# Moving weight conversions, parked stores and late casts within the step order of a retention + two-layer MLP kernel

## The chip, the cores and the metric

One core of one Trainium2 chip runs the whole program. The metric is the device time in microseconds of one execution, as the median over runs. The engines are named as in the profile: PE (matmul), PEld (weight load), DVE (VectorE), ACT (ScalarE), POOL (GpSimd), SP (SyncE, which issues nearly all transfers).

## What is computed

```python
x = attention_with_decay(q, k, v)           # 4 x 8 heads, 576 x 64 each, no softmax
x = x.transpose(0, 2, 1, 3).reshape(2304, 512)
h = x @ w_in                                # 512 -> 2048
x = (h * sigmoid(1.702 * h)) @ w_out        # 2048 -> 512
h = x @ w2_in                               # 512 -> 1024
h = h * softmax(h); h = layer_norm(h) * g_ln
out = h @ w2_out                            # 1024 -> 512
```

## The kernel before

**The stages.** Attention for 16 units of heads comes first, then the first MLP, which the change is about, then the second MLP. Every product of the two MLPs is made of three fp32r matmuls: an operand is held as a rounded part and the rest (`split`: ACT casts, POOL subtracts), and high x high, low x high and high x low are summed.

**The 24 steps.** The first MLP goes through the 2048 hidden columns in four generations `g` of 512. In each generation it goes through three token pairs (768 tokens each, forwards in an even generation, backwards in an odd one), and for each pair through two halves `i` of the generation's columns. This gives the steps s = 6g + 2 * (place of the pair) + i. A step has an h part (`emit_h`) and a y part (`emit_y`). The h part is seven products of six matmuls, in the order A, C, B, A again, C again, D, B again, on four PSUM banks of the ring "s". ACT copies A to c11 (L715) and C to c22 (L719) before the second A and C may be added to the same banks; DVE makes c12 = B + c11 (L707) before the second B. Then come the sums on DVE and four gates, called g11, g12, g21 and g22 in this order: ACT writes the rounded gate and the full one, and POOL (DVE in steps 1 and 3) subtracts them for the low part (L681). The y part is four units of 12 matmuls, each on the 'low' and the 'high' part of one gate. In generation 0 the y parts have other lengths: step 1 has 48 matmuls, step 3 has 72, step 5 has 24. In an even step of the later generations the y part is that of the pair's other half of tokens from the step before, so in these the gates of the step itself are used one step later. DVE adds four finished y banks to memory at the end of a y part (L782).

**The reloading steps.** The operands x of a pair are seven tiles of 768 KB. In the later generations the second step of a pair (7, 9, 13, 15, 19, 21) issues on SP the load of tile j of the next pair (`load_x`, L668) as soon as product j of the pair has read the old one. In steps 1 and 3 the tiles of the next pair are cast and subtracted instead (`split(j)`) and stored to DRAM.

**The background queue.** All weights arrive as 64-bit numbers and have to be made into fp32 by three DVE instructions (`convert`, L276 to L278). These conversions (cost 3), sums of weight blocks on DVE (cost 0.5 for the combinations of the first MLP, L283; cost 1 for those of the second, `v` in `queue_w2in`) and splits stand in one list, `bg`, in a fixed order. A call `slot(n)` takes items from its head until n is used up. An item with a cost that is not ready, because of its `need`, stops the list; an item without cost that isn't ready goes to `held` and is looked at again in the next call. Items marked late run at the head of a later call, at most three (LATE) in each. A split marked "spill" makes an operand of the second MLP in a parking tile (`park`), and its store to DRAM goes out on SP at the end of the call; one such store is allowed in a call, and none while `quiet` is set. A conversion also issues on SP, behind itself, the load of the piece after next into the buffer that it has read (L262), so a load waits on SP until its conversion is done, and what is issued on SP after it waits as well.

**The calls.** In each step there is `slot(0)` behind g11 in the middle of the h part, `slot(pace(s, 0))` at the end of the h part ("h slot" below) and `slot(pace(s, 1))` at the end of the y part ("y slot"). `pace` is a table for the first six steps (PACE), and after that spreads the rest of the list over the calls in proportion to a table `most` with a row for each step of a generation. Before step 23 `flush` calls `slot(9)` until all is done. A conversion writes to a PSUM bank of ring "s", or of ring "y" where `ring` or `psum` says so.

Of the kernel before, what the change touches and what calls it, by code (L numbers as in the profile page):

```python
# [21 lines left out]
DM = H * D  # L22
# [87 lines left out]
_M = {}  # L110
# [44 lines left out]
class Build:  # L155
# [141 lines left out]
    def slot(self, n):  # L297


        late, self.late, i = self.late, [], 0  # L300
        for x in late:
            fn, give, spill = x
            if i >= LATE or (spill and (self.quiet or len(self.stores) > self.last)):
                self.late.append(x)
                continue
            if fn is not None:
                fn()
                i += 1
            self.done.add(give)
        ready = lambda need: all(x in self.done for x in need)  # L310
        wait, self.held = self.held, []
        for x in wait:
            if ready(x[2]):
                self.begin(*x)
            else:
                self.held.append(x)
        while self.bg:
            cost, _, need, _, _ = self.bg[0]
            if cost and (n <= 0 or not ready(need)):
                break  # L320
            x = self.bg.pop(0)
            if ready(need):
                self.begin(*x)
                n -= cost
            else:
                self.held.append(x)
        for fn in self.stores:
            fn()
        self.stores = []
# [16 lines left out]
    def pace(self, s, part):  # L346


        if s < len(PACE):
            return PACE[s][part]  # L350
        most = lambda t, b: ((6, 3), (6, 0), (6, 3), (6, 0), (6, 6), (6, 6))[t % 6][b]
        room = sum(most(t, b) for t in range(s, NSTEP - 1) for b in range(2) if (t, b) >= (s, part))
        return min(most(s, part), -(-self.left() * most(s, part) // room)) if room else 0

# [93 lines left out]
    def queue_w2in(self, c):  # L448

        s = lambda k: self.at(W2_AT[k], DM)  # L450
        before = lambda k: (("r", c - 1, k),) if c else ()
        for k in W2IN:
            self.next_raw(W2_AT[k], before(k))
        v = lambda o, a, b, need=(): self.add(1, lambda: self.sub(s(o), s(a), s(b)), need)
        v(4, 1, 0, before(4) + before(5))
        v(1, 3, 1)
        self.queue_spill(("b11", c), s(0), ("b11", c))
        self.queue_spill(("b22", c), s(3), ("b22", c))
        self.queue_spill(("t1", c), s(4), ("r", c, 5))
        self.queue_spill(("t3", c), s(1), ("r", c, 1))  # L460
        v(0, 3, 4, (("b11", c),))
        self.add(0, lambda: self.done.add(("r", c, 4)))
        v(3, 2, 0, (("b22", c),))
        self.queue_spill(("b21", c), s(2), ("r", c, 2))
        self.queue_spill(("t2", c), s(0), ("r", c, 0))
        self.queue_spill(("t4", c), s(3), ("r", c, 3))


    def un(self, u):
# [215 lines left out]
    def emit_h(self, s):  # L685
# [4 lines left out]
        n = 2 * g + i  # L690
# [35 lines left out]
        yield 2  # L726
        mul(A, 3, "b21", False, True)
        g11(A)
        self.slot(0)
        yield 3  # L730
        mul(C, 4, "b22", False, True)
        add(C, C, c12)
# [203 lines left out]
    def prepare(self):  # L936
# [6 lines left out]
        for i in range(2):  # L943
            self.wo[i] = slot(self.wop, f"wo{i}", SLICE, F32R)
        late_in = [slot(self.wop, f"wo{i}", SLICE, U32) for i in (2, 3)]
# [35 lines left out]
        self.add(0, lambda: swap("win1"))  # L981
        self.queue_convert(late_in[0], _M["stg"], (("in", 0),), None, self.ybank)
        self.queue_in(1, (), slice(0, 1))
        self.queue_convert(late_in[1], _M["stg"] + DM, (("in", 0),))
        self.queue_combine()
        self.add(0, lambda: [swap(2), swap(3)])
        self.queue_in(1, (), slice(1, 3))
# [14 lines left out]
    def run(self):  # L1002
# [15 lines left out]
        def load_w():  # L1018
            dst, piece = self.first_loads.pop(0)
            self.load_raw(dst, self.source(piece))  # L1020
# [22 lines left out]
        for k in range(NPAIR):  # L1043
# [4 lines left out]
            if k == 0:  # L1048
                pt, ends, o = self.bank("T0"), None, []
# [28 lines left out]
            else:  # L1078
# [5 lines left out]
                o, ends = [self.bank(f"o{u}")], [self.bank(f"e{k}")]  # L1084
# [34 lines left out]
        for g, p, i in STEPS:  # L1119
            s = 6 * g + 2 * PAIRS[g].index(p) + i  # L1120
# [7 lines left out]
            for j in self.emit_h(s) if s else chain([0], steps):  # L1128
                while s == 0 and self.first_loads:
                    load_w()  # L1130
                if s == 0:
                    self.store_x(p, j)
                if s == 1 and j == 3:
                    for fn in sums[2:]:
                        fn()
                if s == 2 and j == 4:
                    sums, split = self.combine_x(PAIRS[0][2])
                    for fn in sums:
                        fn()
                if i and after is not None:  # L1140
                    if g == 0:
                        split(j)
                        self.store_x(after, j)
                    else:
                        self.load_x(after, j)
# [31 lines left out]
            self.done.add(("y", s))  # L1177
            self.ring = self.bank if g == 0 and i == 0 else self.ybank
            self.quiet = g > 0 and i == 0 and at + 1 < NPR
            self.slot(self.pace(s, 1))  # L1180
            self.quiet, self.ring = False, self.bank
            if s == 0:
                self.slot(0)
        for fn in y1[:6] + y2[:4]:
            fn()
        self.emit_y(GENS - 1, PAIRS[-1][-1], 1, range(NF - FG, NF))
# [125 lines left out]
```

## Time and profile before

| | |
|---|---|
| median of 3 runs | 670.05 us (669.88 to 671.6) |
| profiled execution | 669.62 us, span 667.8 us |
| PE busy | 647.0 us (97%) |
| DVE, ACT, POOL busy | 447.0 us (67%), 284.5 us (43%), 306.4 us (46%) |
| mean granted clock of PE | 0.992 |
| first step of the first MLP to first matmul of the second | 63.46 to 464.43 us |
| transfers | 121.78 MB, mean 182 GB/s |

Times in the trace count from the start of the span. Busy PE means that matmuls are under way; at a lower granted clock the same matmuls are busy for longer. Granted clock 1.00 is the level of 2.4 GHz, and a mean between 0.5 and 1 over a stretch means that a part of it was run at 1.2 GHz.

### The profile page before, as it was taken

Reading aid. Unit: us, or ns where it says so; the run is one execution under the profiler, and the core shown is the slowest. Engines: PE = TensorE matmul, PEld = TensorE weight load, DVE = VectorE, ACT = ScalarE, POOL = GpSimd, SP = SyncE. Lnnn points to the kernel's source line nnn. Section 1 sums busy time; section 2 is a strip of 40 time slices with the busy share of each in tenths; the row PEclk is TensorE's granted clock in tenths of the full one; section 3 lists DMA queues with packets and bytes.
Section 4 is the critical chain, followed back from the end, with each engine's and each line's share of the span. In section 5 each row is a group of like instructions: output and inputs, shape, how many; then the busy total and the mean of one; then the engine's idle time right before and its main releaser. Section 6 shows DMA issues by size and latency. Waiting matters only on the chain.

```text
span 667.8 us, 11310 instructions
## 1 busy us (share of the span) xinstructions
PE 647.0 (97%) x4326; PEld 601.6 (90%) x4326; DVE 447.0 (67%) x744; ACT 284.5 (43%) x614; POOL 306.4 (46%) x314
## 2 busy tenths in 40 slices
PE   9998989899999999999999999899999999999998
PEld 8997979899999989999999989899888888888887
DVE  3789868737657557557566535345798987887780
ACT  3564553835434324334434434242445433543331
POOL 3687584867246625354735434234244322431200
PEclk9998989899999999999999999999999999999999
DMA  8999356472495943494932584759400000000001
GB/s 348 418 418 373 142 205 252 165 262 66 155 354 198 348 172 97 151 368 164 406 106 85 175 357 164 325 163 365 201 17 32 18 17 31 33 17 16 32 31 49
DMA packets 30006, 121.78 MB, mean 182 GB/s; under 512 B 3328, under 2 KB 3840, under 8 KB 29952
## 3 DMA queue, kind: packets, MB, share of 16 engines
q1 hardware_dynamic: 29808, 120.99, 47.8%
q8 instruction: 34, 0.56, 0.3%
q14 instruction: 20, 0.16, 0.1%
q10 hardware_dynamic: 144, 0.07, 0.0%
HBM read 88.28 MB, written 32.77 MB: 181 GB/s over the span
## 4 chain that ended last, share of the span: by engine, by line
PE 80%; DVE 8%; DMA 8%; issue 2%; ACT 2%; SPq 0%; DVEq 0%; ACTq 0%
PE y L773 23%; PE o L927 15%; PE h L837 13%; DMA x<-xd 8%; PE h_B L701 6%; PE h_A L701 6%; PE h_C L701 6%; DVE mem L283 3%; PE h_D L701 3%; PE zT L901 2%; PE s L570 2%; PE o L585 1%; DVE mem L575 1%; PE warm L1013 1%; PE T L534 1%
## 5 line engine op out<-in xcount | busy, mean ns | idle before, releaser
L681 POOL TENSOR_TENSOR g<-mem,g 128x384 fp32r<-128x384 f32 x86 | 89.4, 1054 | 161.3 <-ACT mem L680 161.2
L292 POOL TENSOR_TENSOR win<-mem,win 128x256 fp32r<-128x256 f32 (+2 forms) x59 | 53.6, 934 | 56.1 <-ACT win L291 52.0
L773 PE MATMUL y<-g,wo 128*128 128x384 f32 x432 | 78.0, 334 | 0.0
L773 PEld LDWEIGHTS y<-g,wo 128*128 128x128 f32 x432 | 75.1, 188 | 0.3 <-DVE mem L782 0.2
L707 DVE TENSOR_TENSOR mem<-h_B,mem 128x384 f32<-128x384 f32 x48 | 26.7, 556 | 64.7 <-PE h_B L701 63.5
L782 DVE TENSOR_TENSOR mem<-y,mem 128x384 f32<-128x384 f32 x76 | 38.5, 551 | 35.5 <-PE y L773 35.2
L283 DVE TENSOR_TENSOR mem<-mem 128x256 f32<-128x256 f32 (+2 forms) x49 | 42.9, 905 | 7.1 <-POOL ws L292 6.4
L292 POOL TENSOR_TENSOR ws<-mem,ws 128x512 fp32r<-128x512 f32 (+1 forms) x32 | 36.8, 1159 | 18.4 <-ACT ws L291 14.2
L715 ACT COPY mem<-h_A 128x384 f32<-128x384 f32 x24 | 11.5, 479 | 77.9 <-PE h_A L701 77.9
L658 POOL TENSOR_TENSOR x<-mem,x 128x384 fp32r<-128x384 f32 x42 | 43.5, 1070 | 0.0
L837 PE MATMUL h<-ut,win 128*128 128x512 f32 x168 | 42.9, 391 | 0.0
L888 POOL TENSOR_TENSOR mem<-mem 128x1 f32<-128x1 f32 x18 | 10.3, 572 | 68.8 <-DVE mem L887 62.6
L927 PE MATMUL o<-u,zs 128*128 128x512 f32 (+1 forms) x171 | 41.7, 388 | 0.0
L773 PE MATMUL y<-g,wo0dt.float32r 128*128 128x384 f32 x216 | 40.3, 334 | 0.0
L773 PE MATMUL y<-g,wo1dt.float32r 128*128 128x384 f32 x216 | 40.3, 334 | 0.0
L927 PE MATMUL o<-wo,zs 128*128 128x512 f32 (+1 forms) x171 | 40.0, 378 | 0.0
L843 DVE TENSOR_TENSOR mem<-h,mem 128x512 f32<-128x512 f32 x36 | 24.6, 687 | 22.4 <-PE h L837 12.5
L773 PEld LDWEIGHTS y<-g,wo0dt.float32r 128*128 128x128 f32 x216 | 37.7, 188 | 0.0
L773 PEld LDWEIGHTS y<-g,wo1dt.float32r 128*128 128x128 f32 x216 | 37.7, 188 | 0.0
L837 PEld LDWEIGHTS h<-ut,win 128*128 128x128 f32 x168 | 31.4, 188 | 6.4
L927 PEld LDWEIGHTS o<-wo,zs 128*128 128x128 f32 x171 | 31.0, 188 | 6.0
L927 PEld LDWEIGHTS o<-u,zs 128*128 128x128 f32 x171 | 29.9, 189 | 5.2
(154 smaller groups left out, 1518.2 us busy)
## 6 DMA issues: line engine op xcount, KB each, us to landing
x<-xd SPq DMA_DIRECT2D x42, 768.0 KB, 8.9
xd<-x SPq DMA_DIRECT2D x21, 768.0 KB, 3.7
mem<-in_w SPq DMA_DIRECT2D x28, 512.0 KB, 4.9
in<-in_att SPq DMA_DIRECT2D x16, 576.0 KB, 7.7
in<-in_att SPq DMA_DIRECT2D x16, 544.0 KB, 8.0
out<-mem SPq DMA_DIRECT2D x17, 256.0 KB, 2.0
mem<-in_w2in SPq DMA_DIRECT2D x8, 512.0 KB, 3.8
wdt<-ws SPq DMA_DIRECT2D x8, 512.0 KB, 8.4
```

The source lines that it names most:

```text
L283: self.nc.vector.tensor_tensor(o, a, b, ALU.subtract)
L292: self.nc.gpsimd.tensor_tensor(lo, src, f32(hi), ALU.subtract)
L570: nc.tensor.matmul(s[a][:, c * CH:(c + 1) * CH], t[h, k:k + CH], self.q(t, c, h), start=True, stop=True)
L658: (engine or self.nc.gpsimd).tensor_tensor(x[:, 1, k], a[:, k], f32(x[:, 0, k]), ALU.subtract)
L681: engine.tensor_tensor(gs[:, 1], u, f32(gs[:, 0]), ALU.subtract)
L701: nc.tensor.matmul(o, w[:, c:c + P], x[j][:, m, k], start=(start and i == 0), stop=(stop and i == 5), skip_group_check=True,)
L707: add = lambda o, a, b: nc.vector.tensor_tensor(o, a, b, ALU.add)
L773: nc.tensor.matmul(o[m], w[:, c:c + P], gs[:, b], start=(begin and i == 0), stop=(end and i == 2),)
L782: nc.vector.tensor_tensor(y[:, m], o[m], y[:, m], ALU.add)
L837: nc.tensor.matmul(o, a[:, l, k], w[:, m], start=(start and i == 0), stop=(stop and i == 5), skip_group_check=True,)
L843: add = lambda o, a, b: nc.vector.tensor_tensor(o, a, b, ALU.add)
L927: nc.tensor.matmul(o[:, 0:n], z[:, a, k], w[:, b, p * n:(p + 1) * n], start=(k == 0 and i == 0), stop=(k == FB - 1 and i == 2),)
```

## The change

Five things are changed. Items of cost 1 no longer stop the list: a sum that isn't ready is held like the items without cost, and the names that the spills and sums of `queue_w2in` wait for are given by the sums themselves. The table `most` has 0 in place of 3 for the y slots of the first and the third step of a generation. The calls behind g11 are quiet, so they make no spill. In generation 0 the y slots of steps 2 and 4 are left out, and of step 0's two calls at the end the second goes to step 1, behind the second product. The conversion of the second late input piece uses ring "y".

```diff
@@ slot
-            if cost and (n <= 0 or not ready(need)):
+            if cost and cost != 1 and (n <= 0 or not ready(need)):
                 break
@@ pace
-        most = lambda t, b: ((6, 3), (6, 0), (6, 3), (6, 0), (6, 6), (6, 6))[t % 6][b]
+        most = lambda t, b: ((6, 0), (6, 0), (6, 0), (6, 0), (6, 6), (6, 6))[t % 6][b]
@@ queue_w2in
-        v = lambda o, a, b, need=(): self.add(1, lambda: self.sub(s(o), s(a), s(b)), need)
+        def v(o, a, b, need=(), give=None):
+            self.add(1, lambda: self.sub(s(o), s(a), s(b)), need, give)
+
         v(4, 1, 0, before(4) + before(5))
         v(1, 3, 1)
...
-        v(0, 3, 4, (("b11", c),))
-        self.add(0, lambda: self.done.add(("r", c, 4)))
-        v(3, 2, 0, (("b22", c),))
-        self.queue_spill(("b21", c), s(2), ("r", c, 2))
-        self.queue_spill(("t2", c), s(0), ("r", c, 0))
-        self.queue_spill(("t4", c), s(3), ("r", c, 3))
+        v(0, 3, 4, (("b11", c),), ("r", c, 4))
+        v(3, 2, 0, (("b22", c), ("r", c, 4)), ("v", c))
+        self.queue_spill(("b21", c), s(2), ("r", c, 2), (("v", c),))
+        self.queue_spill(("t2", c), s(0), ("r", c, 0), (("v", c),))
+        self.queue_spill(("t4", c), s(3), ("r", c, 3), (("v", c),))
@@ emit_h
         g11(A)
+        self.quiet = True
         self.slot(0)
+        self.quiet = False
@@ prepare
-        self.queue_convert(late_in[1], _M["stg"] + DM, (("in", 0),))
+        self.queue_convert(late_in[1], _M["stg"] + DM, (("in", 0),), None, self.ybank)
@@ run, in the loop over the products of a step
+                if s == 1 and j == 1:
+                    self.slot(0)
@@ run, end of a step
-            self.slot(self.pace(s, 1))
+            if s not in (2, 4):
+                self.slot(self.pace(s, 1))
             self.quiet, self.ring = False, self.bank
-            if s == 0:
-                self.slot(0)
```

## Rows read from the trace of the kernel before

**Rows 1.** Windows, each from one step's first matmul to the next's: steps 1, 3, 5, 9, 10, 16, 20, 22

```profile
core 0: us, PE busy (x) PEld busy (x) DVE busy (x) ACT busy (x) POOL busy (x), PEclk, DMA share, GB/s
83.88:105.72 21.84, 19.19 (x91) 16.99 (x91) 14.03 (x20) 12.22 (x24) 19.20 (x17) 0.92 0.65 251
117.16:141.42 24.26, 21.90 (x116) 21.16 (x115) 15.61 (x24) 15.52 (x31) 21.93 (x20) 0.93 0.54 217
152.86:165.81 12.95, 11.74 (x68) 11.43 (x68) 9.40 (x16) 6.87 (x15) 9.81 (x9) 1.00 0.26 81
212.71:228.31 15.60, 15.60 (x92) 15.60 (x92) 11.61 (x20) 7.74 (x16) 14.64 (x12) 1.00 0.75 271
228.31:247.31 19.00, 16.63 (x92) 15.43 (x92) 7.81 (x15) 4.34 (x10) 4.00 (x4) 1.00 0.68 272
325.31:342.21 16.90, 16.08 (x91) 15.50 (x91) 7.79 (x15) 4.34 (x10) 7.24 (x7) 1.00 0.72 289
389.01:406.62 17.61, 16.33 (x92) 15.46 (x91) 6.74 (x13) 4.35 (x10) 3.98 (x4) 1.00 0.64 257
422.22:440.31 18.09, 16.32 (x91) 15.45 (x91) 6.73 (x13) 5.69 (x12) 5.28 (x5) 1.00 0.53 216
```

**Rows 2.** Timeline of PE: product groups after a wait, in steps 1, 3, 5, 10

```profile
89.38 1.79 PE L701 MATMUL h_A<-x,win1dt.float32r 128*128 128x384 f32 x6 [1.84 <-ACT mem L715]
...
123.08 1.48 PE L701 MATMUL h_A<-x,win1dt.float32r 128*128 128x384 f32 x6 [2.06 <-ACT mem L715]
...
157.35 1.34 PE L701 MATMUL h_A<-x,win1dt.float32r 128*128 128x384 f32 x6 [1.21 <-ACT mem L715]
...
237.87 1.28 PE L701 MATMUL h_B<-x,win 128*128 128x384 f32 x6 [0.56 <-DMA x<-xd]
```

**Rows 3.** Windows over the 24 matmuls that follow the first three of these waits

```profile
89.38:95.21 5.83, 5.83 (x25) 5.83 (x26) 3.04 (x4) 4.03 (x7) 5.83 (x6) 0.71 0.67 246
123.08:128.94 5.86, 5.86 (x25) 5.76 (x25) 2.24 (x5) 5.86 (x11) 5.86 (x6) 0.71 0.44 149
157.35:161.65 4.30, 4.30 (x25) 4.30 (x26) 1.29 (x3) 2.58 (x6) 4.20 (x4) 1.00 0.39 122
```

**Rows 4.** Timeline of SP: x loads of step 7; weight load and x loads of step 9

```profile
182.74 2.40 SPq L668 DMA_DIRECT2D x<-xd  x3
...
216.59 0.33 SPq L262 DMA_DIRECT2D mem<-in_w  x1
217.01 2.25 SPq L668 DMA_DIRECT2D x<-xd  x3
```

**Rows 5.** DMA issues: the x load issued at 222.62, us to landing last

```profile
x<-xd SPq DMA_DIRECT2D x1, 768.0 KB, 15.1
```

**Rows 6.** Timeline of DVE: sums in steps 6, 8 and 11; conversion and c12 in step 12

```profile
179.08 1.41 DVE L283 TENSOR_TENSOR mem<-mem 128x512 f32<-128x512 f32 x2
...
208.29 4.36 DVE L283 TENSOR_TENSOR mem<-mem 128x256 f32<-128x256 f32 x4
...
248.27 0.75 DVE L283 TENSOR_TENSOR mem<-mem 128x256 f32<-128x256 f32 x2
...
263.87 0.68 DVE L276 TENSOR_SCALAR conv<-mem 128x512 uint32<-128x512 uint32 x1
...
268.25 0.55 DVE L707 TENSOR_TENSOR mem<-h_B,mem 128x384 f32<-128x384 f32 x1
```

**Rows 7.** Timeline of ACT: casts in step 1; scaling of a parked operand in step 22

```profile
88.33 0.62 ACT L291 CAST wo3dt.float32r<-mem 128x512 fp32r<-128x512 f32 x1 [1.51 <-DVE mem L278]
...
90.32 1.58 ACT L656 CAST x<-mem 128x768 fp32r<-128x768 f32 x2
...
435.97 0.73 ACT L290 ACTIVATE mem<-mem 128x512 f32<-128x512 f32 x1 [0.95 <-DVE mem L278]
```

**Rows 8.** Timeline of POOL: low part of g11 in step 4; weight splits in step 5

```profile
146.73 1.02 POOL L681 TENSOR_TENSOR g<-mem,g 128x384 fp32r<-128x384 f32 x1 [6.11 <-ACT mem L680]
...
153.05 1.48 POOL L292 TENSOR_TENSOR win0dt.float32r<-mem,win0dt.float32r 128x512 fp32r<-128x512 f32 x1
...
156.48 3.09 POOL L292 TENSOR_TENSOR win0dt.float32r<-mem,win0dt.float32r 128x768 fp32r<-128x768 f32 x2 [1.95 <-ACT win0dt.float32r L291]
```

## The prediction

> **What bounds the kernel now.** I read the page first: PE is busy nearly all the time, so only its gaps, and matmuls at a lower clock, can be won. I then cut the first MLP into windows from one step's first matmul to the next's. A step without a loss takes 15.60 us for 90 matmuls, 0.173 us each, and PE is busy in all of it [rows 1]; a product of six takes 1.04. Against this count, step 1 (90 matmuls) loses 6.2 us, step 3 (114 matmuls, 19.8 us) loses 4.5 and step 5 (66 matmuls, 11.4 us) loses 1.5. Steps 10, 16, 20 and 22 lose 3.40, 1.30, 2.01 and 2.49 us, together 9.20 [rows 1]. The other later steps were at 15.6 in the timeline. The two groups have different causes.
>
> In steps 1, 3 and 5 the second A waits 1.84, 2.06 and 1.21 us for ACT's copy of the first A [rows 2]. ACT is late since weight casts stand in front of the copy, and these wait for DVE: the cast of wo3 ended its wait for a conversion at 88.33 [rows 7]. Behind the first two waits PE also ran slower: 24 matmuls took 5.83 and 5.86 us at a granted clock of 0.71, so part of them at the 1.2 GHz level, and behind the third 4.30 at 1.00 [rows 3]. 24 at full rate are 4.16, so the clock cost 1.67 and 1.70, and nothing to speak of behind the 1.21 wait.
>
> In the other four, PE waits for x, as at 237.87 [rows 2]. These loads went out one step earlier. Step 7 begins 31.2 us (two steps) before 212.71, at 181.5, and its first x load goes out at 182.74, 1.2 us in; in step 9 it goes out at 217.01, 4.3 us in, just behind a weight load that SP could issue only at 216.59 [rows 1, 4]. The last x load of step 9 was issued at 222.62 and landed 15.1 later, at 237.7 [rows 5]: 20.7 us from the first issue to the last landing. The second B of step 10, which needs it, was due 15.60 + 6 x 1.04 = 21.84 us after the start of step 9, at 234.55. Started at 1.2 us, the same transfers end at 21.9 even at step 9's slow rate. So the late start decides, and behind it that a conversion stands in front of the x loads on SP.
>
> **Where the change puts things.** I followed the list by its rules through all 24 steps. (1) The y slots of steps 8, 14, 18 and 20, which converted one piece each in front of steps 9, 15, 19 and 21, convert nothing. Their pieces go into h slots (steps 9, 14, 19, 21), behind the x loads on SP or finished before them, and the stores that g11's slot put between x loads go to later slots. (2) The late casts in front of steps 1, 3 and 5 run behind the second product (step 1) or behind g11 (steps 3 and 5). (3) What was spread has to go somewhere: the h slot of step 10 gets four combinations where it had two, the y slot of step 10 two conversions, the y slot of step 11 two conversions and two sums, the h slot of step 12 two conversions behind a sum that waits for POOL, and the last two conversions reach step 22, one in each slot. The parked operand of the very last piece is therefore made in the flush in front of step 23, where the flush was empty before.
>
> **Costs.** *Reloads:* x starts at about 1.2 us in steps 9, 15, 19 and 21, so all four losses go: -9.20. Step 13 had a clean start; now two weight loads stand in front of it, the second issued about 2 us in, which puts its x loads at about 3 us. With 18 to 19 us to the last landing (step 9's 20.7 with a 512 KB store among them) that is 21 to 22 against 21.84: 0, at most 1.9 with the full 20.7.
>
> *Step 1:* the copies and x casts pass the wo3 cast, but everything that follows on ACT (x casts, g11, and behind them DVE's sums and g12) still waits for the same conversion. In the old order the copy of A, one x cast and the copy of C lie between wo3's cast, whose next instruction starts about 0.5 after it, and the x casts at 90.32 [rows 7]; 90.32 - 88.85 = 1.47 is what the chain wins. The wait of PE moves from the h part to the y part, where g12 is late, and with it the lower clock. I take -1.4 out of 6.2; bounds 0 and -3.1, the chain's 1.47 plus the 1.67 of the clock.
>
> *Step 3:* the wait of 2.06 and the 1.70 of clock go. D's bank is that of step 2's last conversion, which ends some 0.3 us behind the time at which D would be due: -3.76 + 0.3 = -3.45.
>
> *Step 5:* the three casts now stand on POOL between g11's low part and g12's. The low part of g11 starts 5.31 into a step (146.73 in step 4, which began at 141.42) [rows 1, 8]. Then 1.02 + 1.48 + 3.09 + 1.02 give 11.9 at step 5's own prices [rows 8]. The y part of step 5 needs g12's low at 7.28 + 2.08 + 0.69 = 10.05. PE waits 1.85, and a little less where POOL is alone, say 1.7, in place of the 1.5 lost now: +0.2. The cover that a y part gives elsewhere (three units, 6.2 us) is missing in this short one. A wait of 1.7 is nearer to 1.84, which cost the clock, than to 1.21, which didn't [rows 2, 3]: +1.7 (bounds 0 and 1.7).
>
> *DVE between steps 10 and 13:* in step 12 (start 247.31 + 15.60 = 262.91) two conversions ran in front of c12 from 263.87 to 268.25, and c12 ended at 268.80, in time for the second B due at 269.15 [rows 1, 6]. Two sums of 512 columns, 1.41 [rows 6], now stand between: c12 ends at 270.2, +1.1. Step 11 gets the same two conversions behind two more combinations, which take 0.75 to 2.2 (two at 0.75, four at 4.36) [rows 6]; some of that is covered by the wait for y's last bank: 0 to 0.7, I take 0.5.
>
> *Step 23:* the conversion in front of it starts 0.96 into the step and ends about 2.2 later [rows 6], at 3.2. ACT then scales (0.73) and casts (about 0.5 to the next start) [rows 7], and copies A: 4.9 to 5.0. The second A is due at 3.12, so PE waits 1.8: +1.8, and by the row of the 1.84 wait +1.7 of clock [rows 2, 3]. SP's store of that piece holds up the loads of the second MLP's weights by some 6 us; these have the 17 us of two y parts as cover, and cost nothing unless they are held beyond that.
>
> *Nothing:* the quiet call in the other steps, the held sums (DVE stands idle in front of c12 in most steps), and step 0's bank of ring "y", whose gain of some 0.6 us ends in step 1's wait for the same conversions.
>
> **Sum:** -9.20 - 1.4 - 3.45 + 0.2 + 1.7 + 1.1 + 0.5 + 1.8 + 1.7 = -7.05. From the profiled execution's 669.62 that gives 662.6; the median of the runs is 0.43 above that execution, so 663.0.
>
> **Rivals.** *A, the new waits cost no clock:* in steps 5 and 23 PE waits but goes on at 2.4 GHz, as behind the wait of 1.21. That speaks for it in step 5, the 1.84 row against it in step 23. Both: 663.0 - 3.4 = 659.6.
>
> *B, the reload is mended in part:* the x loads start early, but the weight loads and stores now bunched in h slots get between them or in front, as in step 13. If half of the 9.20 stays, 667.6. Against it speaks that step 7 starts clean behind the same kind of h slot.
>
> *C, slower:* the casts behind g11 make POOL late for g12 in steps 9, 11 and 17 too, as in step 5. There the y part needs g12's low only after three units, at 7.28 + 6.24 = 13.5, and POOL should be through by 11 to 12; it decides from 1.5 to 2.5 us of further lateness on. Each place would cost a wait and clock of about 3.4, so three make 663.0 + 10.2 = 673.2. What could make POOL late is work of DVE beside it: four sums took 4.36 us in step 8, where two took 0.75 in step 11 [rows 6]. The Trainium skill (GPSIMD Engine Reference, 8. Key points) says that GpSimd shares its SBUF interfaces with VectorE and contends with its instructions of two SBUF inputs, as these sums are. By that rule the casts put into the same stretch as DVE's work would stretch each other and rival C would be the outcome; the sums' rows agree that such a stretch occurs, but its size there, 2.9 us over four sums, was without loss to PE in step 9 [rows 1].
>
> *D, no change:* if SP is held by something else than the conversion (the store in front of the weight load), the x loads start no earlier, and -9.20 falls away while the new waits stay: 672. The clean start of step 7 speaks against it.
>
> **How the numbers follow.** A difference under 0.3% (2 us) can't be told from none. Forecast 0.58, with a range of its own from 660.5 to 665.5: the clock of one place, step 1's bound, step 13's. A 0.20. B 0.10. C 0.06, D 0.06. Faster by over 2 us is all of the forecast and of A and nearly all of B: 0.87. Within 2 us: the worse part of B, 0.04. Slower: most of C and D, 0.09. The range from 658.0 to 668.0 leaves out C and D and the best ends of A.
>
> **What would show it.** Right: no wait of PE for x in steps 10, 16, 20 and 22 and steps of 15.6 us there; step 3 at about 20.8; x loads 1.2 us into steps 9, 15, 19 and 21; a wait of about 1.8 for ACT in the second A of step 23 and one of about 1 in the second B of step 12; in step 5 a wait in the y part for POOL's g. Wrong: the second A of step 23 on time, or waits of PE for POOL in steps 9, 11 or 17; x loads of step 9 still behind a late weight load.

## The result and the profile after

The changed kernel takes 662.27 us (median of 4 runs, 661.43 to 663.43) against 669.96 of the kernel before on the same chip (669.42 to 671.6): ratio 0.9882, 95% interval 0.9859 to 0.9905. Its profiled execution took 662.16, span 660.4, at a mean granted clock of 0.997.

The first view is again windows from one step's first matmul to the next's, of steps 1, 3, 5, 9 to 12, 14, 22 and 23 (columns as in [rows 1]):

```profile
core 0: us, PE busy (x) PEld busy (x) DVE busy (x) ACT busy (x) POOL busy (x), PEclk, DMA share, GB/s
82.66:103.33 20.67, 17.91 (x91) 17.19 (x92) 14.25 (x20) 12.23 (x24) 19.72 (x17) 0.92 0.71 266
114.77:135.81 21.04, 20.48 (x115) 19.69 (x115) 14.91 (x24) 15.32 (x31) 19.52 (x18) 1.00 0.55 213
147.25:160.69 13.44, 11.71 (x67) 11.39 (x67) 10.34 (x18) 7.24 (x16) 8.35 (x8) 1.00 0.27 84
207.53:223.12 15.59, 15.59 (x91) 15.59 (x91) 8.71 (x16) 6.39 (x14) 11.12 (x10) 1.00 0.97 373
223.12:238.72 15.60, 15.60 (x91) 15.60 (x91) 10.03 (x15) 5.89 (x13) 8.00 (x7) 1.00 0.64 246
238.72:255.44 16.72, 15.90 (x91) 15.58 (x91) 14.15 (x24) 6.10 (x13) 8.66 (x8) 1.00 0.43 140
255.44:272.75 17.31, 15.88 (x91) 15.56 (x91) 12.36 (x19) 5.37 (x12) 6.96 (x6) 1.00 0.27 82
288.35:306.00 17.65, 16.34 (x91) 15.46 (x91) 13.03 (x24) 7.13 (x15) 11.01 (x10) 1.00 0.74 277
...
415.20:430.80 15.60, 15.60 (x91) 15.60 (x91) 6.73 (x13) 5.69 (x12) 5.30 (x5) 1.00 0.42 171
430.80:456.92 26.12, 24.40 (x140) 23.81 (x139) 15.95 (x29) 9.90 (x23) 12.29 (x14) 1.00 0.74 284
```

Against [rows 1], steps 10 and 22 are at 15.60, as are 16 and 20: the 9.20 us of the reloads are gone. Step 3 is 3.2 us shorter than its 24.26. Steps 11, 12, 14 and 23, which had no loss, now wait, and steps 1 and 5 wait at another place than before. The timeline of PE after shows where:

```profile
95.36 3.91 PE L776 MATMUL y<-g,wo3dt.float32r 128*128 128x384 f32 x12 [2.26 <-ACT g L679]
...
159.20 1.66 PE L776 MATMUL y<-g,wo3dt.float32r 128*128 128x384 f32 x8 [1.73 <-POOL g L682]
...
245.95 1.34 PE L702 MATMUL h_B<-x,win0dt.float32r 128*128 128x384 f32 x6 [0.82 <-DVE mem L708]
...
263.28 1.31 PE L702 MATMUL h_B<-x,win1dt.float32r 128*128 128x384 f32 x6 [1.43 <-DVE mem L708]
...
294.76 1.29 PE L702 MATMUL h_D<-x,win1dt.float32r 128*128 128x384 f32 x6 [0.56 <-DMA x<-xd]
...
435.81 1.34 PE L702 MATMUL h_A<-x,win1dt.float32r 128*128 128x384 f32 x6 [1.72 <-ACT mem L716]
```

They are the y part of step 1 (the gate's wait of 2.26), the y part of step 5, c12 in steps 11 and 12, the x of step 14, and the second A of step 23. Windows over the matmuls behind the first, second and last of these waits, to be held against [rows 3]:

```profile
95.36:99.30 3.94, 3.94 (x14) 3.94 (x15) 3.29 (x5) 3.94 (x8) 3.94 (x4) 0.57 0.91 381
159.20:163.40 4.20, 4.20 (x24) 4.20 (x25) 2.17 (x4) 3.41 (x8) 3.14 (x3) 1.00 0.57 169
435.81:439.98 4.17, 4.17 (x24) 4.17 (x25) 1.10 (x2) 2.07 (x5) 2.15 (x3) 1.00 0.41 136
```

Only behind step 1's wait is a part run at 1.2 GHz. Steps 5 and 23 go on at 2.4 GHz.

The timeline of SP after: the x loads of step 9, then in step 13 a store and the x loads behind it.

```profile
208.76 6.56 SPq L669 DMA_DIRECT2D x<-xd  x7
...
276.32 0.42 SPq L432 DMA_DIRECT2D wdb<-ws  x1
276.83 5.78 SPq L669 DMA_DIRECT2D x<-xd  x7
```

Step 9 (start 207.53) issues its first x load 1.23 us in; in step 13 (start 272.75), behind two weight loads and a store, it is 4.08.

The lengths of the steps of all kernels that were run, in us, from the same windows; a dot is 15.60 to 15.65, and steps left out (2, 4, 7, 9, 15, 17 to 19, 21) have no loss in any.

| kernel | 0 | 1 | 3 | 5 | 6 | 8 | 10 | 11 | 12 | 13 | 14 | 16 | 20 | 22 | 23 |
|---|---|---|---|---|---|---|---|---|---|---|---|---|---|---|---|
| before | 20.41 | 21.84 | 24.26 | 12.95 | 15.70 | · | 19.00 | · | · | · | · | 16.91 | 17.61 | 18.09 | 24.11 |
| after | 18.72 | 20.66 | 21.05 | 13.44 | · | · | · | 16.72 | 17.31 | · | 17.65 | · | · | · | 26.11 |
| u1 | 20.19 | 20.92 | 21.02 | 13.46 | · | · | · | · | 17.33 | 19.90 | 16.53 | · | · | · | 24.11 |
| u2 | 20.06 | 20.90 | 21.04 | 13.46 | · | 16.62 | 17.24 | · | 17.17 | 15.79 | 19.26 | · | · | · | 26.13 |
| u3 | 18.74 | 20.67 | 21.05 | 13.46 | · | · | 18.34 | · | 15.75 | · | · | 16.81 | 17.59 | 19.04 | 24.09 |
| u4 | 19.27 | 21.84 | 24.27 | 12.95 | 15.70 | · | 16.31 | · | · | · | · | · | · | · | 24.09 |
| u5 | 20.21 | 20.87 | 21.03 | 13.44 | · | · | 18.06 | · | · | · | · | · | 16.15 | · | 24.11 |
| f1 | 18.75 | 20.80 | 21.05 | 13.46 | · | · | · | 16.70 | 17.33 | · | 17.65 | · | · | · | 24.11 |
| f2 | 20.06 | 20.88 | 21.03 | 13.46 | · | · | · | · | · | · | · | · | · | · | 26.11 |
| f3 | 20.28 | 20.90 | 21.03 | 11.44 | 16.25 | · | · | 16.73 | 17.31 | · | 17.39 | · | · | · | 26.11 |
| f4 | 19.97 | 22.46 | 21.07 | 13.46 | · | · | · | 16.71 | 17.31 | · | 17.46 | · | · | · | 26.09 |
| f5 | 18.73 | 23.60 | 21.03 | 11.44 | 16.24 | · | · | · | · | · | · | · | · | · | 24.11 |
| f6 | 21.17 | 17.30 | 21.03 | 13.46 | · | · | · | 16.73 | 17.31 | · | 17.32 | · | · | · | 26.11 |
| f7 | 18.74 | 17.28 | 21.03 | 11.44 | 16.27 | · | · | · | · | · | · | · | · | · | 24.11 |

Step 0 changes by 1.1 to 1.6 us between executions whatever the edit, and by 2.4 in f6; the last section comes to it. So a difference of that size between two medians is read from the steps.

### The profile page after: what moved, and what is told of

The parts are those of the page before. It is cut to its first block, busy times and chain, and to the rows that moved or that the text cites. A ratio compares the mean times of both kernels' runs of the same rounds, so it can differ in the third digit from the quotient of the medians.

```text
span 660.4 us, 11306 instructions
## 1 busy us (share of the span) xinstructions
PE 642.1 (97%) x4326; PEld 600.3 (91%) x4326; DVE 446.4 (68%) x744; ACT 283.6 (43%) x614; POOL 305.2 (46%) x314
## 4 chain that ended last, share of the span: by engine, by line
PE 80%; DVE 11%; issue 3%; DMA 2%; POOL 1%; ACT 1%; DVEq 0%; POOLq 0%; ACTq 0%
PE y L776 25%; PE o L930 15%; PE h L840 13%; PE h_B L702 6%; PE h_A L702 6%; PE h_C L702 5%; DVE mem L283 3%; PE h_D L702 3%; PE zT L904 2%; DMA x<-xd 2%; PE s L571 2%; PE o L586 1%; DVE mem L576 1%; DVE conv L277 1%; DVE conv L276 1%
## 5 line engine op out<-in xcount | busy, mean ns | idle before, releaser
L283 DVE TENSOR_TENSOR mem<-mem 128x256 f32<-128x256 f32 (+2 forms) x49 | 46.4, 982 | 12.0 <-POOL ws L292 11.3
```

What stands on the lines that cost most here:

```text
L283: self.nc.vector.tensor_tensor(o, a, b, ALU.subtract)
```

## Experiments

Two groups: u1 to u5 take the change apart, f1 to f7 try its new waits. Diffs of u1, u2 and f1 to f7 are against the changed kernel, those of u3 to u5 against the kernel before. Ratios are to the kernel before on the same chip.

**u1: the old table back.**

```diff
-        most = lambda t, b: ((6, 0), (6, 0), (6, 0), (6, 0), (6, 6), (6, 6))[t % 6][b]
+        most = lambda t, b: ((6, 3), (6, 0), (6, 3), (6, 0), (6, 6), (6, 6))[t % 6][b]
```

> The changed kernel with the old table of work after a step's y part, so that a step in front of a reloading one may convert again; everything else stays changed. By the rules of the queue a conversion that also issues a weight load then stands in front of the x loads of steps 7, 9, 15 and 19; the one in front of step 21 issues no weight load, in front of step 13 there are four combinations and no load; and the last spill leaves before step 23. Theory (SP waits at the weight load for the conversion's end, and the x loads stand behind it): steps 8, 10, 16 and 20 lose about what before's steps 10, 16 and 20 lost (3.4, 1.3, 2.0 us; between 1 and 3.5 us each), step 22 loses nothing, step 14's 2.05 us falls as its load comes in another place, step 23 wins back its 2.0 us; about 662.3 + 4 x 2 - 4 = 666 us. Rival 1 (the conversions themselves, by VectorE's time, held the x loads): step 22 loses its 2.5 us too, 668 us. Rival 2 (the spills' stores between the x loads were the cause): no step loses, 658 us.

664.06 us (662.7 to 666.18), ratio 0.9893 [0.9826, 0.9960]. The theory fell. The conversion and its weight load stand in front of the x loads again, as the timeline of SP in step 9 (start 209.50) shows, and step 10 lost nothing; neither did 8, 16 and 20. So far rival 2 holds.

```profile
212.63 0.33 SPq L262 DMA_DIRECT2D mem<-in_w  x1
213.05 4.61 SPq L669 DMA_DIRECT2D x<-xd  x7
```

What it lost instead was in step 13, where the four combinations stood on DVE in front of c12, and PE waited 2.46 us and then ran on at the lower level:

```profile
282.49 2.24 PE L702 MATMUL h_B<-x,win 128*128 128x384 f32 x6 [2.46 <-DVE mem L708]
```

The 0.93 that step 14 lost is not for x either: the last x landed 3.84 us into the step, and the longest wait of PE there, 0.64 at its second A, was for ACT's copy.

**u2: spills, and with them stores, let in behind g11 again.**

```diff
-        self.quiet = True
         self.slot(0)
-        self.quiet = False
```

> The changed kernel without the rule that holds spills back at the place behind the first gate. One store then stands between the x loads again in steps 7, 9, 13, 19 and 21 (in before there were up to two in some), while no conversion stands in front of them. Theory (the weight load behind a conversion was the cause, a store only adds its own time on the DMA engines, about 1.2 us): steps 8, 10, 20 and 22 lose 0 to 0.5 us each, step 14's 2.05 us grows by up to 1.2 us; 662 to 664 us. Rival (the stores between the x loads held them back): half or more of 3.4, 2.0 and 2.5 us returns in steps 10, 20 and 22; 666 us or more.

665.88 us (663.4 to 667.57), ratio 0.9938 [0.9913, 0.9962]. Steps 20 and 22 stayed clean with a store between the x loads, so the store alone doesn't make the wait either. Step 10 lost 1.64, for x, and step 14 lost 1.6 more than in the changed kernel. In step 9 the first x load was also late there, 3.43 us in, behind another store that SP issued at 3.01. Step 8's 1.02 is not x: its last x came in time, and the longest wait of PE, 0.50 at the first B, was for a conversion on DVE. The timeline of PE in step 10:

```profile
233.24 1.30 PE L702 MATMUL h_B<-x,win 128*128 128x384 f32 x6 [1.28 <-DMA x<-xd]
```

The two runs together give a rule. For each reloading step I took from the trace when its first x load was issued and when its last one landed, both from the step's start, and set beside it what the next step lost:

| kernel, reloading step | first x issue | last x lands | lands - 21.63 | lost |
|---|---|---|---|---|
| before 9 / 15 / 19 / 21 | 4.31 / 4.23 / 3.55 / 3.63 | 25.03 / 22.93 / 23.63 / 24.12 | 3.40 / 1.30 / 2.00 / 2.49 | 3.40 / 1.31 / 2.01 / 2.49 |
| after 9 | 1.23 | 19.43 | below 0 | 0 |
| after 13 | 4.08 | 23.68 | 2.05 | 2.05 |
| u1 9 / 15 / 19 | 3.55 / 3.55 / 3.58 | 20.54 / 20.59 / 20.72 | below 0 | 0 |
| u2 9 | 3.43 | 23.27 | 1.64 | 1.64 |
| u2 19 / 21 | 1.23 / 1.23 | 20.47 / 20.67 | below 0 | 0 |

The limit of 21.63 is fitted to the four rows of before and holds in the others to 0.03. It is the 21.84 of the prediction less 0.21. It holds as closely in u3, in u5 and for step 13 of f1, f3, f4 and f6. Where the reloading step is itself longer than 15.60, as step 13 is in u1 (19.90) and u2 (15.79), the limit moves by the difference. With an early start and nothing between, the last x lands at 17.9 to 19.7 (steps 9, 15, 19, 21 of the changed kernel and f1); a conversion in front puts it at 20.5 to 20.7 (steps 9, 15, 19 of u1), a store between at 20.2 to 21.0 (u2, and steps 7 and 13 of before), and both, as in before, at 22.9 to 25.0.

**u4: the holding back of spills, and with them their stores, alone.** The rule was then tested on the kernel before, with one part of the change:

```diff
         g11(A)
+        self.quiet = True
         self.slot(0)
+        self.quiet = False
```

> The kernel before with one edit of the change alone: the place behind the first gate holds spills back, so that no store stands between the x loads; the conversions and their weight loads stay in front of steps 9, 15, 19 and 21. Theory formed after the first runs (the wait is the time at which the last of seven x transfers lands, about 21.6 us into the reloading step being early enough; a conversion in front and stores between cost it 2 to 3 us each, and it takes both to pass the limit): the first x load is still issued 3.5 to 5.5 us into steps 9, 15, 19 and 21, the last x lands 20.3 to 22.5 us into them, and of the 9.2 us of steps 10, 16, 20 and 22 at most 1 us is left; 669.5 - 8.2 to 9.2 = 660.3 to 661.3 us, if the spills put off cost nothing elsewhere. Rival (the conversion and its weight load alone make the wait): 4 us or more are left, 664 us or more.

660.87 us (660.51 to 662.0), ratio 0.9859 [0.9806, 0.9913]: this one edit gives 8.6 us (669.48 - 660.87), where the whole change gave 7.7. Step 10 kept 0.71 of the 9.2, the others nothing. The timelines of SP in step 9 (start 212.37) and of PE in step 10:

```profile
216.96 0.33 SPq L262 DMA_DIRECT2D mem<-in_w  x1
217.38 3.83 SPq L668 DMA_DIRECT2D x<-xd  x7
```
```profile
234.84 1.28 PE L701 MATMUL h_B<-x,win 128*128 128x384 f32 x6 [0.47 <-DMA x<-xd]
```

The loads start 5.02 us into the step and the last lands at 22.34; 22.34 - 21.63 is the 0.71 that was lost. In steps 15, 19 and 21, also behind a conversion, the last x landed at 20.6 to 21.4 and nothing was lost. Holding a spill back also moves its cast on ACT and its subtraction on POOL, but the landings show the store itself: in u2's step 9 the x loads on either side of a store landed 3.05 us apart (13.91 and 16.96), the next two 1.91 and 1.82 later.

**u3: the edits of steps 0 to 5 alone.**

```diff
-        self.queue_convert(late_in[1], _M["stg"] + DM, (("in", 0),))
+        self.queue_convert(late_in[1], _M["stg"] + DM, (("in", 0),), None, self.ybank)
+                if s == 1 and j == 1:
+                    self.slot(0)
-            self.slot(self.pace(s, 1))
+            if s not in (2, 4):
+                self.slot(self.pace(s, 1))
-            if s == 0:
-                self.slot(0)
```

> The kernel before with the edits that act in steps 0 to 5 alone: nothing behind the y part of steps 2 and 4, step 0's last place moved into step 1, the second late conversion in a y bank. Theory (the terms add up): step 3 wins 3.2 us, step 1 wins 1.2 us, step 0 0.6 to 1.7 us, step 5 loses 0.5 us, the four reloads keep their 9.2 us, and steps 11, 12, 14 and 23 lose nothing; 670.0 - 4.3 to 5.4 = 664.6 to 665.7 us, if the queue behind step 5 stands as it stood. Rival (the moved conversions push the queue later, and the gain of steps 0 to 5 is given back in steps 6 to 23): 667 us or more.

664.49 us (663.27 to 668.08), ratio 0.9936 [0.9913, 0.9958]: as expected. Steps 1, 3 and 5 are as in the changed kernel, the reloads lose 9.4.

**u5: u3 and u4 together**, so the change without its table and without the passing over of sums.

> The kernel before with two parts of the change: spills held back behind the first gate, and the edits of steps 0 to 5. Left out are the new table (conversions still stand in front of a reloading step) and the passing over of waiting sums. Theory (each part acts in its own steps; what the change gave back in steps 11, 12, 14 and 23, 1.12 + 1.71 + 2.05 + 2.0 = 6.9 us, belongs to the two parts left out): steps 0 to 5 as in the changed kernel, step 10 at 15.6 to 16.4 us, steps 11, 12, 14, 16, 20 and 22 at 15.6, step 23 at 24.1; 662.3 - 6.9 + 0.7 = 656.1 us. Rival (the table is needed once steps 0 to 5 are shorter, as step 22 lost 3.4 instead of 2.5 us with those edits alone): 2 us or more come back in steps 10, 16, 20 and 22, 658 us or more.

658.61 us (656.44 to 660.15), ratio 0.9828 [0.9798, 0.9858]. Steps 11, 12, 14 and 23 are clean, as the theory had it, but in the profiled execution, the slowest of the six, steps 10 and 20 lost 2.46 and 0.55, as the rival had it. Step 9's first x load was issued at the same 5.02 as in u4, but the last landed at 24.09 in place of 22.34. With a conversion in front the slack is gone, and the transfers' own time decides, 19.07 us here and 17.32 in u4 from the first issue to the last landing; what made them slower here was not tried. So the table has a use: in the changed kernel the last x of step 9 lands at 19.43. Together with the passed-over sums its price was about 3.7 us there, 662.27 - 658.61 (by the profiled steps 6.9 lost in 11, 12, 14 and 23 against 3.0 in 10 and 20).

**f1: both last conversions in step 22's first half.**

```diff
+        if (s, part) == (NSTEP - 2, 0):
+            return 6
```

> The changed kernel with both of the last two conversions at the end of step 22's first half, so that their spills are scaled and stored behind step 22's y part and nothing is left in front of step 23. Theory (step 23's wait of 1.72 us for the first bank is the last spill's scaling, conversion and its neighbours on ScalarE at the step's head): step 23 falls from 26.11 to 24.1 us and nothing else moves; 660.3 us. Rival (the bank is late for another reason, the split of the next weights' cast or the last gates): no change, 662.3 us; a second rival (the doubled conversions make step 22's gates late): step 22 loses 0.5 to 2 us and the sum stays at 661 to 662.

660.18 us (659.94 to 660.6), ratio 0.9833 [0.9770, 0.9897]. Step 23 fell to 24.11 and nothing else moved. Its wait was the flush: in the changed kernel the timeline of ACT at that place is scaling, cast, then the copy of A for which PE waits.

```profile
434.01 0.72 ACT L290 ACTIVATE mem<-mem 128x512 f32<-128x512 f32 x1 [6.17 <-DVE mem L278]
434.76 0.62 ACT L291 CAST win<-mem 128x512 fp32r<-128x512 f32 x1
435.28 0.47 ACT L716 COPY mem<-h_A 128x384 f32<-128x384 f32 x1
```

**f2: one conversion in place of two in the y slots of steps 10 and 11.**

```diff
+        if (s, part) in ((10, 1), (11, 1)):
+            return 3
```

> The changed kernel with one conversion instead of two behind the y parts of steps 10 and 11; the later conversions move on by one place each, so that step 12's two conversions and their weight loads no longer stand in front of step 13's x loads. Theory (steps 11 and 12 wait at the c12 addition because VectorE still converts and sums behind the y part; step 14 waits because two weight loads and a store hold step 13's first x load to 4.08 us into the step, and its last x lands 23.7 us into it where about 21.6 is early enough): steps 11, 12 and 14 fall to 15.6 us, the last x of step 13 lands 18 to 20 us into the step, and 1.12 + 1.71 + 2.05 = 4.9 us are won, 662.3 - 4.9 = 657.4 us. Rival (the work is only moved: one of steps 12 to 17 now waits for a later conversion): half comes back, about 660 us. Rival 2 (the c12 addition is late because of the y additions in front of it, which stay): steps 11 and 12 stay, 660.2 us.

659.28 us (658.17 to 660.14), ratio 0.9843 [0.9819, 0.9867]. Steps 11, 12 and 14 are clean, 4.9 us by the steps; the median fell by 3.0, with step 0 at 20.06 in the profiled execution where the changed kernel's had 18.72. Step 13's first x load is issued at 1.23 and the last lands at 18.54. The two crowded y slots had made all three waits.

**f3: in step 5 the place behind g11 moved behind g12.**

```diff
-            self.slot(0)
+            if s != 5:
+                self.slot(0)
...
         g12(C)
+        if s == 5:
+            self.slot(0)
```

> The changed kernel with the place behind step 5's first gate moved behind its second, so that GpSimd takes the second gate's low part ahead of the three weight splits (4.65 us). Theory (the wait of 1.73 us in front of step 5's second y part is GpSimd's queue, and the clock was not lowered by it): step 5 falls from 13.44 to 11.5 to 11.7 us, 660.4 us. Rival (the splits are only put in front of the third and fourth gates, whose low parts are then late): step 5 or the head of step 6 keeps 1 us or more, 661.5 us or more.

661.77 us (660.48 to 664.12), ratio 0.9886 [0.9854, 0.9918]. The cause was right: step 5 has no loss left, with GpSimd taking g12's low part before the splits, as its timeline shows.

```profile
155.50 1.02 POOL L682 TENSOR_TENSOR g<-mem,g 128x384 fp32r<-128x384 f32 x1 [0.63 <-ACT mem L681]
156.48 4.69 POOL L292 TENSOR_TENSOR win0dt.float32r<-mem,win0dt.float32r 128x512 fp32r<-128x512 f32 x3
```

Of the 2.0 us, 0.65 came back in step 6, which starts sooner while the weight load for its second conversion lands when it did; DVE waits 1.71 for it, and c12 is late, as the timeline of DVE shows. The rest doesn't show in the median; in the profiled execution step 0 alone was 1.56 us longer than the changed kernel's.

```profile
164.09 0.69 DVE L276 TENSOR_SCALAR conv<-mem 128x512 uint32<-128x512 uint32 x1 [1.71 <-DMA mem<-in_w2in]
```

**f4: step 1's two late operand sums behind g12's sum, in place of ahead of it.**

```diff
-                if s == 1 and j == 3:
+                if s == 1 and j == 4:
```

> The changed kernel with the two last operand sums of step 1 (3.30 us on VectorE) put behind the second gate's sum instead of in front of it. Theory (the gate of the y part's last slice is 2.26 us late because its addition stood behind the two sums on VectorE, and the 12 matmuls behind the wait ran 1.8 us longer at a granted clock of 0.57): wait and clock go, step 1 falls from 20.66 to 16.6 to 17.2 us, 658.4 us. Rival (ScalarE is late with that gate anyway, for the casts of the stored operands in its queue): the wait shrinks to 1 us or more and the clock's part may stay, step 1 at 18.5 to 20 us, 660.5 to 662 us. Rival on the other side (the fifth stored operand, which needs one of the two sums, is late and step 2's operands with it): step 2 or 3 grows by 1 us or more.

666.13 us (665.36 to 667.75), ratio 0.9947 [0.9929, 0.9966]: the theory fell, step 1 grew by 1.8. The second gate was in time, but now the sums stood ahead of D's additions on DVE, and the x casts, which wait for the sums, ahead of the third gate on ACT. The timelines of ACT and PE:

```profile
98.66 2.30 ACT L657 CAST x<-mem 128x768 fp32r<-128x768 f32 x3 [3.94 <-DVE mem L283]
100.86 0.48 ACT L679 ACTIVATE g<-h_D 128x384 fp32r<-128x384 f32 x1
```
```profile
101.39 4.04 PE L776 MATMUL y<-g,wo2dt.float32r 128*128 128x384 f32 x12 [3.97 <-ACT g L679]
```

**f5: f1, f2, f3 and f4 together.**

> The changed kernel with four further edits together: one conversion behind the y parts of steps 10 and 11, both last conversions in step 22's first half, the place behind step 5's first gate moved behind its second, and step 1's two late operand sums behind the second gate's sum. Theory (the four waits are independent): the gains add up, 4.9 + 2.0 + 1.9 + 3.7 = 12.5 us, 649.8 us. Rival (the gain of one is another's wait): 653 us or more.

657.71 us (655.99 to 658.59), ratio 0.9816 [0.9794, 0.9837]. The other gains add up by the steps; f4's part is a loss of 2.9 in place of a gain.

**f6: the sums, and the casts, splits and stores of the last three operands, behind all gates of step 1.**

```diff
-                if s == 1 and j == 3:
-                    for fn in sums[2:]:
-                        fn()
...
-                if i and after is not None:
+                if i and after is not None and not (s == 1 and j > 3):
...
+            if s == 1:
+                for fn in sums[:1:-1]:
+                    fn()
+                for j in (4, 5, 6):
+                    split(j)
+                    self.store_x(after, j)
```

> The changed kernel with step 1's two late operand sums, and the casts, splits and stores of the three operands that step 2 takes last, behind the step's last gate instead of in the middle of its first half. Theory (with the sums in front of the second gate that gate was late, with the sums behind it the third was, since VectorE took the sums and ScalarE the casts ahead of it; behind all four gates they delay no gate): no wait in step 1's y part, step 1 falls from 20.66 to 16.4 to 16.8 us, step 2 starts some 4 us sooner and finds its last three operands just ready, as they have 4 to 6 us more before their products; 658.3 us. Rival (GpSimd's six splits of about 1.05 us each end too late): step 2 or 3 grows by 1 to 3 us; 659.5 to 661.5 us.

658.38 us (657.7 to 660.97), ratio 0.9840 [0.9816, 0.9864]. Step 1 fell by 3.4 us to 17.30 (a wait of 0.42 for a gate's low part is left), and steps 2 and 3 did not grow.

**f7: f1, f2, f3 and f6 together.**

> The changed kernel with the edit of the other kernel of this call in step 1, one conversion behind the y parts of steps 10 and 11, both last conversions in step 22's first half, and the place behind step 5's first gate moved behind its second. Theory (the waits are independent, as the steps of the single edits showed): 4.9 us in steps 11, 12 and 14, 2.0 in step 23, 1.4 in steps 5 and 6, 4.0 in step 1, together 12.3 us less than the changed kernel, with a spread of some 1.5 us for the clock at step 0's first products; 650 to 651.5 us. Rival (step 1's gain comes back in step 2 or 3): 652.5 to 654.5 us.

651.84 us (650.3 to 654.07), ratio 0.9748 [0.9725, 0.9772]: the fastest version, 2.5% below the kernel before and 10.4 us below the changed one by the medians, 11.6 by the profiled executions (662.16 and 650.56). Windows of its steps 1, 5 and 6:

```profile
82.67:99.95 17.28, 16.37 (x91) 15.60 (x91) 12.55 (x20) 10.93 (x21) 13.83 (x13) 1.00 0.68 242
...
143.86:155.30 11.44, 11.44 (x68) 11.44 (x68) 8.43 (x15) 7.11 (x16) 5.75 (x6) 1.00 0.29 92
155.30:171.57 16.27, 15.89 (x92) 15.57 (x91) 12.30 (x20) 6.35 (x15) 8.37 (x8) 1.00 0.46 143
```

## Why the prediction was right, and where it was not

The time forecast was 663.0 and 662.27 was measured. The places were right; several sizes were not, and their errors nearly cancelled, which is luck: one of them is the 1.2 us of step 0, most of it a clock that differs from execution to execution.

| term | predicted | measured by steps |
|---|---|---|
| reloads (10, 16, 20, 22) | -9.20 | -9.2 |
| step 13's x loads (seen in step 14) | 0, at most 1.9 | +2.05 |
| step 1 | -1.4 | -1.18 |
| step 3 | -3.45 | -3.21 |
| step 5 | +0.2, clock +1.7 | +0.49, no clock |
| step 12 | +1.1 | +1.71 |
| step 11 | +0.5 | +1.12 |
| step 23 | +1.8, clock +1.7 | +2.0, no clock |
| step 0 and its start | 0 | -1.2 |

*Reloads.* The amount was right, the reason only half. "So the late start decides, and behind it that a conversion stands in front of the x loads on SP" is refuted by u1, where the start is late and nothing is lost. The prediction had taken the 20.7 us from first issue to last landing as given; without a store between they are 17.0 (u1, step 9: 20.54 - 3.55). Late start and store each cost some 2 us of a slack of 2 to 4 (21.63 less 17.9 to 19.7); u4 shows that taking away the spills with their stores was enough for all but 0.7 us. This also explains why before's steps 7 and 13, with a store and an early start, lost nothing.

*Step 13.* The term that was mis-sized. The x loads started at 4.08 us in place of about 3, since the second weight load waited for a conversion until 3.19, and the last landed 19.6 after the first issue. That lies between the 18 to 19 and the full 20.7 that were taken, and the loss is 0.15 past the bound that went with the earlier start.

*Clock.* "A wait of 1.7 is nearer to 1.84, which cost the clock" failed in step 5, and step 23's 1.72 cost none either: rival A held at both, worth 3.4 us. None of the 15 waits of 1.72 or 1.73 in these two steps, over the changed kernel and the runs, was followed by a lower clock. This paid for what step 13, 11 and 12 cost more.

*Steps 11 and 12.* Both waits were where they were put, and f2 shows that they came from the crowded y slots. In front of step 11's c12 the four combinations took 4.94 us, where at most the 4.36 of [rows 6] was taken; in f2 they took as long and one conversion less left step 11 clean. In step 12 the two sums took 2.10 and not the 1.41 of [rows 6]. The timelines of DVE and POOL after show why the row was the wrong one to price by:

```profile
234.38 4.94 DVE L283 TENSOR_TENSOR mem<-mem 128x256 f32<-128x256 f32 x4
...
260.66 2.10 DVE L283 TENSOR_TENSOR mem<-mem 128x512 f32<-128x512 f32 x2
262.68 0.55 DVE L708 TENSOR_TENSOR mem<-h_B,mem 128x384 f32<-128x384 f32 x1
```
```profile
260.76 1.45 POOL L682 TENSOR_TENSOR g<-mem,g 128x384 fp32r<-128x384 f32 x1 [9.29 <-ACT mem L681]
```

GpSimd ran a gate's low part beside the sums, and that took 1.45 in place of the 1.02 it takes in [rows 8]. So both were stretched. The same shows in the other sums of this trace: 14 of the 32 with 256 columns ran with GpSimd idle and took 0.41 to 0.43 us, and 11 of the 18 that ran beside it took over 1.2. The Trainium skill (GPSIMD Engine Reference, 8. Key points) says that GpSimd shares its SBUF interfaces with VectorE and contends with those of its instructions that have two SBUF inputs. The trace agrees, at 0.7 us for the two sums of step 12. Rival C, which this stretch was to bring about, did not come: PE had no wait for POOL in steps 9, 11 and 17.

*Steps 1, 3, 5.* As predicted: step 1's wait moved from the h part to the y part and kept its lower clock, step 5's wait is 1.73 against 1.7. In step 3 PE waits 0.27 for D's bank, where 0.3 was taken. f3 and f6 show the causes in steps 5 and 1 by taking them away. But the lower clock was not a price of its own in step 1, as the bound of 1.47 + 1.67 had it. In the profiled execution of u3, with the same edits in step 1, PE stayed at 2.4 GHz behind this wait, then waited for the next gates, and the step took 20.67 all the same. Its timeline of PE, and its window to set beside the changed kernel's 95.36 to 99.30 (0.57):

```profile
95.08 2.64 PE L773 MATMUL y<-g,wo3dt.float32r 128*128 128x384 f32 x12 [2.28 <-ACT g L678]
98.06 1.59 PE L773 MATMUL y<-g,wo2dt.float32r 128*128 128x384 f32 x6 [0.34 <-ACT g L678]
```
```profile
95.08:99.00 3.92, 3.56 (x16) 2.64 (x16) 3.30 (x5) 3.92 (x8) 3.92 (x4) 1.00 0.91 379
```

*Step 0.* -1.69, of which the second late conversion's bank is only part. u4 has the old bank and 19.27, the changed kernel 18.72, both with a first product at 2.4 GHz: 0.55 is the bank's. The timeline of PE of u4 shows the wait for it at D, which the changed kernel hasn't:

```profile
72.45 1.32 PE L701 MATMUL h_D<-x,win0dt.float32r 128*128 128x384 f32 x6 [0.59 <-DVE g L681]
```

The rest is the clock at the first product, which differs from execution to execution (next section but one).

What the change was worth by parts: holding back the spills with their stores 8.6 us (u4), the edits of steps 0 to 5 some 5.3 (u3, 669.79 - 664.49). Together the two gave 11.8 and not 13.9 (u5, 670.38 - 658.61), as some of the reloads' loss came back. The table and the passed-over sums cost 3.7 net beside these two (u5), and the waits that they made in steps 11, 12, 14 and 23 went when f1 and f2 spread the crowded slots.

## What to carry to other kernels

A chain of transfers that must end by a time has one number to watch, the landing of the last, and it pays to know the slack before asking which delay "causes" a wait: two delays that each fit into it cost nothing alone. Work taken out of a slot that looks guilty does not vanish; the next slot that receives it should be priced at the same time, with what runs beside it on the other engines. And on an engine that works in order, move work behind the last urgent instruction of its stretch, not behind the next one (f4 and f6).

## What the runs showed of the hardware

In the first MLP the clock of PE was at 1.2 GHz for a stretch behind waits of 1.84 and 2.06 [rows 2, 3], 2.26, 2.46 (u1) and 3.97 us (f4), and stayed at 2.4 GHz behind waits of 1.21 [rows 3], 1.43, 1.72 and 1.73. The length of the wait doesn't settle it: behind the wait of 2.28 in step 1 of u3 it stayed at 2.4 GHz, and behind the same wait, 2.25 to 2.28, it fell in the changed kernel, u1, u2, u5, f1, f2 and f3.

At the first product of step 0 it differed from execution to execution, between the changed kernel and u1 with the same instructions ahead. The timelines of PE of the kernel before, of the changed kernel and of u1:

```profile
63.46 2.29 PE L701 MATMUL h_A<-x,win0dt.float32r 128*128 128x384 f32 x6
```
```profile
63.94 1.31 PE L702 MATMUL h_A<-x,win0dt.float32r 128*128 128x384 f32 x6
```
```profile
64.23 2.29 PE L702 MATMUL h_A<-x,win0dt.float32r 128*128 128x384 f32 x6
```

Six matmuls take 2.29 or 1.31, and step 0 is 1.1 to 1.6 us longer in the first case, 2.4 in f6, where the lower level lasted longer. Of the profiled executions of the kernels with the new bank, five were short (18.72 to 18.75) and seven long (19.97 to 21.17). What decides it was not tried. It is probably a part of why medians of like kernels lie 1 to 2 us apart here; that is not shown.

The seven x transfers of 768 KB land one after another in the order in which SP issued them, weight loads and stores among them, in every trace. With nothing between, the later ones of a step are mostly 1.8 to 1.9 us apart (step 9 of the changed kernel: 12.03, 13.89, 15.73, 17.59 and 19.43), with a store of 512 KB between 3.05 (u2, step 9). So each thing issued ahead pushes back all that follow.
